# Squared-ReLU MLP: last store in two halves on two queues, w2 in three loads, last w1 loads merged

## Chip, cores, metric

One Trainium2 chip, one core, bfloat16. The metric is device time in microseconds (us). Times are quoted as the median of a kernel's runs. Every ratio is the mean time of one kernel's fast runs over the mean of the other's fast runs of the same rounds on the same chip, so it is not quite the ratio of the medians quoted beside it. "Span" is the time from the first to the last instruction in a profile; it is about 2 us shorter than the timed value. PE is TensorE; SPq and ACTq are the DMA queues of SyncE and ScalarE. A DMA is *issued* by its queue and has *landed* when all its bytes are in place, as its semaphore tells.

## The reference

```python
B, S, D, F = 1, 2048, 576, 4608
def reference(x, w1, b1, w2, b2):
    h = einsum("bsd,df->bsf", x, w1) + b1
    r = where(h > 0, h, 0)
    h = r * r
    return einsum("bsf,fd->bsd", h, w2) + b2
```

## The kernel before

The sequence is cut into four blocks of 512 rows. D = 576 is 4.5 times 128, so most of the first matmul is done in pairs: one matmul on partitions 0 to 63 and one on partitions 64 to 127, for two different columns of w1. Such a pair of column tiles is called a *row tile* here; there are 16. A row tile needs 18 matmuls (9 pairs), about 1.94 us (the first twelve run from 9.50 to 32.81 us in the profile).

w1 for these tiles is loaded in pieces. Each load fills 64 partitions, the lower or the upper half, and all are issued in order on SyncE's queue:

```python
    w1_v = w1.rearrange("(c p) f -> p c f", p=H)          # H = 64
    def load_w1(eng, h, j0, j1):
        keep(eng.dma_start(out=w1_h[h * H:(h + 1) * H, :, j0 * P:j1 * P],
                      in_=w1_v[:, :, GW + h * FH + j0 * P:GW + h * FH + j1 * P]))
    # ... cut ...
    W2CH = 18
    def load_w2(c):
        keep(nc.sync.dma_start(out=w2_sb[:, c * W2CH:(c + 1) * W2CH, :],
                               in_=w2_view[:, c * W2CH:(c + 1) * W2CH, :]))
    # ... cut ...
    for (j0, j1) in [(0, 1), (1, 2), (2, 4), (4, 6), (6, 8), (8, 10), (10, 12)]:
        load_w1(nc.sync, 0, j0, j1)
        load_w1(nc.sync, 1, j0, j1)
    load_xT(1)                                  # DMA transposes of x, block 1
    for (j0, j1) in [(12, 14), (14, 16)]:       # four loads of 288 KB
        load_w1(nc.sync, 0, j0, j1)
        load_w1(nc.sync, 1, j0, j1)
    # ... cut: b2 as a column (b2_col) and as rows (b2_bc) ...
    for c in range(2):
        load_w2(c)
    load_xT(2)
    alloc_hT(0)
    a_full(0, "k_outer")
    a_rows(0, 12, 1)                            # row tiles 0 to 15 of block 0
```

The end of the kernel stores the last 128 rows in two column pieces; only the second, 128 x 128 (32 KB), is stored after all other work:

```python
                keep(nc.vector.tensor_tensor(out=o_sb[:, d0:d1], in0=po[:, 0:d1 - d0], in1=b2_bc[:, d0:d1], op=ALU.add))
                keep(nc.sync.dma_start(out=out2[rt * P:(rt + 1) * P, d0:d1], in_=o_sb[:, d0:d1]))
```

## Time and profile before

| what | value |
|---|---|
| time, median of the first 3 runs (of 6 with those beside the changed kernel) | 290.89 us (290.85) |
| span of the profile | 288.7 us |
| PE busy | 284.6 us, 99% |
| last add ends | 286.42 us |
| tail after it | 2.3 us |

From the page of the kernel before, busy times by engine, and the chain that ended last by engine:

```profile
PE 284.6 (99%) x2027; PEld 138.9 (48%) x2032; DVE 78.6 (27%) x177; ACT 96.5 (33%) x152; POOL 0.9 (0%) x7
...
PE 97%; DMA 1%; SPq 0%; issue 0%; DVE 0%
```

TensorE bounds the kernel: it is busy for 284.6 of 288.7 us. So a DMA matters here only where PE waits for it, or after PE has finished.

The timeline of TensorE around the start of row tile 12 in block 0, kernel before. Columns: start in us, duration in us, engine, line, operation, output and inputs, shapes, count. L181 is the lower matmul of a pair, L183 the upper:

```profile
32.60 0.38 PE L181 MATMUL ph<-xTw,w_h 64*128 64x512 bf16 x1
32.60 0.38 PE L183 MATMUL ph<-xTw,w_h 64*128 64x512 bf16 x1
32.81 0.38 PE L181 MATMUL ph<-xTw,w_h 64*128 64x512 bf16 x1
32.82 0.38 PE L183 MATMUL ph<-xTw,w_h 64*128 64x512 bf16 x1
33.03 0.38 PE L181 MATMUL ph<-xTw,w_h 64*128 64x512 bf16 x1
```

Pairs start every 0.215 us. Tile 12 begins at 32.81 without a gap.

The timeline of SyncE's queue at the same place (issue times of DMAs; the four w1 loads are one merged row):

```profile
23.88 2.65 SPq L82 DMA_DIRECT2D w_h<-in_w_dram  x4
26.58 1.06 SPq L285 DMA_DIRECT2D b_col<-in_b_dram  x1
27.68 1.62 SPq L288 DMA_DIRECT2D b_bc<-in_b_dram  x1
```

The same four loads by tile (the issue's duration in ns, min/median/max, and starts; then the time from issue to landing):

```profile
L82 SPq DMA_DIRECT2D w_h<-in_w_dram x4: 609/636/638, 23.9 to 25.9; - x4
...
DMA to landing us min/median/max: 6.7/7.0/7.2
```

The trace has a landing for the last three of the four: 31.2, 32.4 and 32.9 us (start of issue plus time to landing). While they flow, between 26 and 30 us, the DMAs move 258 GB/s. The columns of this view: the stretch, its length, busy us (and instructions) of PE, weight loads, VectorE, ScalarE and GpSimd, the granted clock, the DMA engines' share, GB/s:

```profile
26.00:30.00 4.00, 4.00 (x40) 1.76 (x38) 1.82 (x5) 2.65 (x5) 0.00 (x0) 1.00 1.17 258
```

The timeline of the end, kernel before:

```profile
286.13 0.29 DVE L274 TENSOR_TENSOR o_sb<-po,b_bc 128x128 bf16<-128x128 f32 x1 [1.52 <-PE po L272]
286.45 0.33 SPq L275 DMA_DIRECT2D out_dram<-o_sb  x1
```

The store landed 1.5 us after its issue began; the closing semaphores bring the end to 288.7 us.

### The profile page before, as it was taken

The page shows a single profiled execution, that of the slowest core. Times are in us where ns is not written, and L with a number is a line of the kernel's source. Part 1 is how long each engine was busy: PE and PEld are TensorE (multiplying, and loading weights), DVE is VectorE, ACT ScalarE, POOL GpSimd, SP SyncE. Part 2 cuts the span into 40 slices and gives each one's busy share as a digit, 9 for nine tenths or more (in the row PEclk, how much of TensorE's full clock was granted, in tenths as well). Part 3 has the DMA queues.
Part 4 walks back from the last instruction along what each step waited for, and adds up shares of the span by engine and source line. Part 5 has one row for each costly group of instructions (what it writes and reads, how often), then busy time and mean ns, then how long its engine had stood idle before and what let it go on. Part 6 is the DMA issues. An engine that isn't in the chain of part 4 may idle for free.

```text
span 288.7 us, 4690 instructions
## 1 busy us (share of the span) xinstructions
PE 284.6 (99%) x2027; PEld 138.9 (48%) x2032; DVE 78.6 (27%) x177; ACT 96.5 (33%) x152; POOL 0.9 (0%) x7
## 2 busy tenths in 40 slices
PE   8999999999999999999999999999999999999996
PEld 5544444444444555555544444444444455555555
DVE  3444544444500200000025444444440001100001
ACT  3666666666500000000027666666670000000000
POOL 0000000000000000000000000000000000000000
PEclk9999999999999999999999999999999999999999
DMA  6999999600001100000000000000000110000000
GB/s 198 236 244 197 265 388 246 94 0 2 0 18 36 37 16 18 16 16 18 16 16 2 1 2 0 2 0 2 0 2 0 36 39 16 16 16 19 32 17 18
DMA packets 31573, 16.59 MB, mean 57 GB/s; under 512 B 15552, under 2 KB 31552, under 8 KB 31552
## 3 DMA queue, kind: packets, MB, share of 16 engines
q1 hardware_dynamic: 30928, 15.72, 22.3%
q10 hardware_dynamic: 624, 0.57, 0.7%
q8 instruction: 16, 0.26, 0.4%
q14 instruction: 5, 0.04, 0.0%
HBM read 11.43 MB, written 2.36 MB: 48 GB/s over the span
## 4 chain that ended last, share of the span: by engine, by line
PE 97%; DMA 1%; SPq 0%; issue 0%; DVE 0%
PE ph L181 42%; PE po L272 38%; PE pt L253 11%; PE pn L202 4%; DMA w1n<-in_w_dram 1%; PE pn L217 1%; PE ph L183 1%; PE pn L196 1%; SPq L72 0%; DVE o_sb L274 0%; PE b1T_ps L159 0%; PE pn L198 0%
## 5 line engine op out<-in xcount | busy, mean ns | idle before, releaser
L181 PE MATMUL ph<-xTw,w_h 64*128 64x512 bf16 x576 | 124.6, 376 | 0.0
L183 PE MATMUL ph<-xTw,w_h 64*128 64x512 bf16 x576 | 124.6, 376 | 0.0
L272 PE MATMUL po<-w_sb,hT 128*128 128x448 bf16 (+2 forms) x612 | 109.4, 341 | 0.0
L169 ACT ACTIVATE r<-ph,b1T 128x512 bf16<-128x512 f32 x128 | 81.1, 685 | 41.6 <-PE ph L183 41.6
L181 PEld LDWEIGHTS <-w_h 64*128 64x128 bf16 x576 | 54.1, 94 | 68.3
L272 PEld LDWEIGHTS <-hT 128*128 128x128 bf16 x612 | 58.5, 98 | 51.0
L170 DVE TENSOR_TENSOR hT<-r 128x512 bf16<-128x512 bf16 x144 | 61.2, 426 | 76.9 <-ACT r L169 76.9
L183 PEld LDWEIGHTS <-w_h 64*128 64x128 bf16 x576 | 54.1, 94 | 0.0
L274 DVE TENSOR_TENSOR o_sb<-po,b_bc 128x448 bf16<-128x448 f32 (+2 forms) x17 | 10.2, 597 | 125.8 <-PE po L272 125.8
L253 PE MATMUL pt<-hT,w_sb 128*128 128x512 bf16 x142 | 31.3, 379 | 0.1
L169 ACT ACTIVATE r<-pn,b1T 128x512 bf16<-128x512 f32 x16 | 10.3, 688 | 62.0 <-PE pn L198 60.6
L253 PEld LDWEIGHTS <-w_sb 128*128 128x128 bf16 x144 | 14.1, 98 | 17.0
L256 ACT ACTIVATE oT<-pt,b2T 128x512 bf16<-128x512 f32 x4 | 2.7, 687 | 28.3 <-PE pt L253 28.3
L202 PE MATMUL pn<-xTw,w1n 128*128 128x512 bf16 x45 | 10.4, 379 | 0.4 <-issue 0.3
L202 PEld LDWEIGHTS <-w1n 128*128 128x128 bf16 x48 | 4.5, 98 | 6.0 <-issue 0.8
L217 PE MATMUL pn<-xTw,w1n 128*128 128x256 bf16 x32 | 3.7, 273 | 0.1
L63 PE MATMUL wps<-const-bfloat16-1.0 128*128 128x512 bf16 (+1 forms) x7 | 2.9, 597 | 0.8 <-PEq L328 0.8
L217 PEld LDWEIGHTS <-w1n 128*128 128x128 bf16 x32 | 3.0, 98 | 0.6 <-DMA w1n<-in_w_dram 0.3
L115 DVE COPY xTw<-xTw 64x2048 bf16<-64x2048 bf16 x4 | 2.8, 690 | 0.6 <-ACT xTw L152 0.5
L116 DVE COPY xTw<-xTw 64x2048 bf16<-64x2048 bf16 x4 | 2.8, 688 | 0.1
L196 PE MATMUL pn<-xTw,w1n 64*128 64x512 bf16 x8 | 2.4, 379 | 0.0
L198 PE MATMUL pn<-xTw,w1n 64*128 64x512 bf16 x8 | 2.4, 379 | 0.0
(21 smaller groups left out, 10.5 us busy)
## 6 DMA issues: line engine op xcount, KB each, us to landing
w_sb<-in_w_dram SPq DMA_DIRECT2D x2, 2592.0 KB, 15.2
w_h<-in_w_dram SPq DMA_DIRECT2D x14, 288.0 KB, 6.6
out_dram<-o_sb SPq DMA_DIRECT2D x15, 112.0 KB, 1.7
w_h<-in_w_dram SPq DMA_DIRECT2D x4, 144.0 KB, 3.2
out_dram<-ot SPq DMA_DIRECT2D x4, 128.0 KB, 2.0
x_sb<-in_x_dram ACTq DMA_DIRECT2D x2, 144.0 KB, 3.0
x_sb<-in_x_dram SPq DMA_DIRECT2D x2, 144.0 KB, 3.0
w1n<-in_w_dram ACTq DMA_DIRECT2D x2, 128.0 KB, 3.6
```

The source lines that it names most:

```text
L63: keep(nc.tensor.matmul(wps[:, 0:n], lhsT=ones[:, 0:P], rhs=ones[:, 0:n], start=True, stop=True))
L115: keep(nc.vector.tensor_copy(out=xT[0:H, SPC:SPC + 4, :], in_=xT[H:P, E3:E3 + 4, :]))
L169: keep(nc.scalar.activation(out=r[:], in_=bank[:], func=ACT.Relu, bias=b1T[:, ft:ft + 1], scale=1.0))
L170: keep(nc.vector.tensor_tensor(out=hTs[sb][:, ft, :], in0=r[:], in1=r[:], op=ALU.mult))
L181: keep(nc.tensor.matmul(bx[:], lhsT=w1_h[0:H, LO_C[i], jc], rhs=xT[0:H, LO_W[i], :], start=(i == 0), stop=(i == NC - 1)))
L183: keep(nc.tensor.matmul(by[:], lhsT=w1_h[H:P, UP_C[i], jc], rhs=xT[H:P, UP_W[i], :], start=(i == 0), stop=(i == NC - 1)))
L196: keep(nc.tensor.matmul(banks[2 * i][:], lhsT=w1n8[0:H, 2 * i * P:(2 * i + 1) * P], rhs=xT[0:H, SPC, :], start=start, stop=stop, skip_grou ...
L202: keep(nc.tensor.matmul(banks[g][:], lhsT=w1n[:, k, g * P:(g + 1) * P], rhs=xT[:, O + k, :], start=start, stop=stop))
L217: keep(nc.tensor.matmul(banks[g][:, hc], lhsT=w1n[:, k, g * P:(g + 1) * P], rhs=xT[:, O + k, hc], start=(h == 0 and k == 0), stop=False, s ...
L253: keep(nc.tensor.matmul(pt[:], lhsT=w2_sb[:, ft, DM:D], rhs=hT[:, ft, :], start=(i == 0), stop=(i == NFT - 1)))
L272: keep(nc.tensor.matmul(po[:, 0:d1 - d0], lhsT=hT[:, ft, jj * P:(jj + 1) * P], rhs=w2_sb[:, ft, d0:d1], start=(i == 0), stop=(i == NFT - 1)))
L274: keep(nc.vector.tensor_tensor(out=o_sb[:, d0:d1], in0=po[:, 0:d1 - d0], in1=b2_bc[:, d0:d1], op=ALU.add))
```

## The change

Intent: issue fewer and larger w1 loads, spread w2 over three loads, and let two queues share the last store.

```diff
-    W2CH = 18
+    W2CH = 12
@@ last store
-                keep(nc.sync.dma_start(out=out2[rt * P:(rt + 1) * P, d0:d1], in_=o_sb[:, d0:d1]))
+                if last and rt == S // P - 1 and d1 == DM:
+                    for h, eng in enumerate((nc.sync, nc.scalar)):
+                        rows = slice(rt * P + h * H, rt * P + (h + 1) * H)
+                        keep(eng.dma_start(out=out2[rows, d0:d1], in_=o_sb[h * H:(h + 1) * H, d0:d1]))
+                else:
+                    keep(nc.sync.dma_start(out=out2[rt * P:(rt + 1) * P, d0:d1], in_=o_sb[:, d0:d1]))
@@ loads
-    for (j0, j1) in [(12, 14), (14, 16)]:
+    for (j0, j1) in [(12, 16)]:
         load_w1(nc.sync, 0, j0, j1)
         load_w1(nc.sync, 1, j0, j1)
@@
-    for c in range(2):
+    for c in range(3):
         load_w2(c)
```

## The prediction

> **What bounds the kernel now.** TensorE. The engine summary gives PE 284.6 us busy of a 288.7 us span (99%); the chain of waits puts 97% on PE and 1% on a DMA (first weight loads, 1.7 to 5.4 us). In the timeline matmuls follow one another every 0.215 us from 9.5 us on; the list of waits shows no PE wait on a DMA after 5.4 us. The last add ends at 286.42 us; then comes a tail of 2.3 us: the store is issued at 286.45 (0.33 us on SyncE's queue), lands 1.5 us after its issue began (the tile's DMA view), near 287.95, and closing semaphores take it to 288.7.
>
> The change touches DMAs only: it can gain only in that tail, and lose only by making PE wait.
>
> **1. Last store split (128 x 128, 32 KB).** Nearly all of the 1.5 us is fixed: stores of 112 KB land in 1.7 us. The DMA engines are busy 15% of the one microsecond in which this store moves. Two halves move the same bytes. [...] ScalarE is idle then, so the halves start together. But the two 64-partition loads of 64 KB took 0.58 us to issue, against 0.44 for 128-partition loads of 128 KB, and the end now waits for two landings. Estimate: +0.05 us, between -0.1 and +0.3.
>
> **2. w1 row tiles 12 to 15 in two loads of 576 KB instead of four of 288 KB.** The only place where PE could be made to wait. The four are issued from 23.88 to 26.52 us and land at about 30.6, 31.7, 32.4 and 32.9 us. Row tile 12 starts on PE at 32.81 us; it needs only the first two, with 1.1 us to spare. Merged, it needs all; landing as now, PE would wait about 0.1 us. But contiguous runs grow from 512 to 1024 bytes. With the DMA engines full, the 512-byte phase moves 234 to 292 GB/s (26 to 30 us) and the 1152-byte rows of w2 366 to 390. At an estimated 340 GB/s the 1.18 MB that start flowing at 26 us take 3.5 us instead of 4.5 to 5, so the last lands near 31 to 32 us. Expected PE wait 0; at worst about 0.5 us. SyncE saves about 1.3 us of issue, worth nothing.
>
> **3. w2 in three loads of 1.73 MB instead of two of 2.6 MB.** Now landed at about 41.2 and 48.2 us; the first matmul that reads w2 runs at 75.4. One issue more (0.4 us), same bytes and rows. Worth 0.
>
> **Sum.** 290.89 + 0.05 (tail) + 0.05 (small chance of a wait at tile 12) = 291.0 us, range 290.3 to 291.7, mostly the spread of the runs before (290.7 to 291.53). Chances: faster by over 2% 0.5%, within 2% 98.5%, slower by over 2% 1%.
>
> **What would show it.** Right: PE busy and chain the same within 0.5 us; row tile 12's first matmul at about 32.8 us without a wait; both w1 loads landed before it; w2 landed before 50 us; two stores near 286.5, each landing in 1.4 to 1.7 us, span ending 2.2 to 2.5 us after the last add. Wrong: a PE gap before tile 12; a tail under 2.1 us (halves do land sooner) or over 2.7.
>
> **What would make it wrong.** Merged loads landing after 33.3 us[...]; other waits reordered by the new number of transfers.

The sum as forecast: 290.89 + 0.05 + 0.05 = 291.0 us (290.99).

## The result

292.03 us median of 6 runs (291.65 to 292.75), against 290.85 (290.7 to 291.53) before: ratio 1.0038, 95% interval 1.0022 to 1.0054. That is about 1.1 us slower. It is within 2%, as forecast, but it lies above the forecast range of 290.3 to 291.7.

The page after, busy by engine and the chain that ended last:

```profile
PE 285.3 (98%) x2032; PEld 139.1 (48%) x2032; DVE 78.6 (27%) x177; ACT 96.5 (33%) x152; POOL 1.0 (0%) x7
...
PE 87%; SPq 6%; DMA 4%; issue 0%; ACTq 0%; DVE 0%
```

The chain no longer runs through PE alone: it now passes through SyncE's queue and a DMA.

TensorE at row tile 12, after. The bracket is idle time before the instruction and what ended it:

```profile
32.66 0.38 PE L181 MATMUL ph<-xTw,w_h 64*128 64x512 bf16 x1
32.67 0.38 PE L183 MATMUL ph<-xTw,w_h 64*128 64x512 bf16 x1
32.88 0.38 PE L181 MATMUL ph<-xTw,w_h 64*128 64x512 bf16 x1
33.74 0.39 PE L183 MATMUL ph<-xTw,w_h 64*128 64x512 bf16 x1 [0.49 <-DMA w_h<-in_w_dram]
33.75 0.39 PE L181 MATMUL ph<-xTw,w_h 64*128 64x512 bf16 x1
```

The upper matmul of the first pair should have started with its lower partner at 32.88. It started at 33.74: **0.86 us lost**. The bracket shows only 0.49, because it counts from the modelled end of the matmul before; start-to-start distances are the safer reading.

SyncE's queue, after:

```profile
24.21 1.29 SPq L82 DMA_DIRECT2D w_h<-in_w_dram  x2
25.54 0.63 SPq L290 DMA_DIRECT2D b_col<-in_b_dram  x1
26.22 0.61 SPq L293 DMA_DIRECT2D b_bc<-in_b_dram  x1
```

The second merged load was issued at 24.86 and took 8.8 us, so it landed at 33.7 us, when PE resumed:

```profile
L82 SPq DMA_DIRECT2D w_h<-in_w_dram x1: 633/633/633, 24.9 to 24.9; - x1
...
DMA to landing us min/median/max: 8.8/8.8/8.8
```

The loads did not move faster than before's four, as the prediction had hoped, but slower:

```profile
26.00:30.00 4.00, 4.00 (x40) 1.82 (x38) 1.79 (x5) 2.65 (x5) 0.00 (x0) 1.00 0.99 222
```

The end, after:

```profile
287.06 0.29 DVE L274 TENSOR_TENSOR o_sb<-po,b_bc 128x128 bf16<-128x128 f32 x1 [1.52 <-PE po L272]
287.38 0.56 SPq L278 DMA_DIRECT2D out_dram<-o_sb  x1
287.39 0.56 ACTq L278 DMA_DIRECT2D out_dram<-o_sb  x1
```

Each issue takes 0.56 us instead of 0.33. Both landings, from one view:

```profile
DMA to landing us min/median/max: 1.8/1.9/2.1
```

The SyncE half lands after 1.8 us, the ScalarE half after 2.1, and the span ends at 290.3: a tail of 3.0 us instead of 2.3.

So the profiled runs differ by 1.6 us (290.3 against 288.7), made of 0.86 at tile 12, about 0.65 in the tail, and 0.07 in the start-up. The medians differ by 1.2 us. That fits waits that vary from run to run, but only one run of this kernel was profiled. Two of the signs that the prediction had named as "wrong" are there: a PE gap before tile 12 and a tail over 2.7 us.

### The profile page after: what moved, and what is told of

It is laid out like the page before. It is cut to its first block, busy times and chain, and to the rows that moved or that the text cites. A ratio compares the mean times of both kernels' runs of the same rounds, so it can differ in the third digit from the quotient of the medians.

```text
span 290.3 us, 4696 instructions
## 1 busy us (share of the span) xinstructions
PE 285.3 (98%) x2032; PEld 139.1 (48%) x2032; DVE 78.6 (27%) x177; ACT 96.5 (33%) x152; POOL 1.0 (0%) x7
## 4 chain that ended last, share of the span: by engine, by line
PE 87%; SPq 6%; DMA 4%; issue 0%; ACTq 0%; DVE 0%
PE po L272 38%; PE ph L181 21%; PE ph L183 14%; PE pt L253 11%; SPq L82 4%; PE pn L202 4%; DMA w_h<-in_w_dram 3%; SPq L122 2%; DMA w1n<-in_w_dram 1%; SPq L123 0%; PE pn L196 0%; ACTq L72 0%; PE pn L198 0%; DVE o_sb L274 0%
```

## The experiments

Each kernel is the kernel before with only the edit shown, except where said. "Tail" is always the span's end minus the end of the last add.

### One part at a time

**Split store alone** (only the store hunk of the change).

> The kernel before with the last store alone split. Theory T (the split store itself costs): the end comes about 2.95 us after the last add instead of 2.28, so the kernel is 0.5 to 0.7 us slower than before, and no wait of PE on a w1 load. Rival (the loss is all in the loads): tail 2.3 us, time within 0.15 us of before.

Measured: 291.54 us against 291.01, ratio 1.0024 (1.0011 to 1.0037). The tail was 3.0 us; PE waited for no w1 load. So the split store by itself costs about 0.6 us. The rival fell.

**Merged w1 alone** (only the `(12, 16)` hunk).

> The kernel before with the last w1 loads alone merged. Theory W (tile 12 now waits for both merged loads): the upper load lands at 33.3 to 33.9 us, PE waits 0.5 to 1.0 us before row tile 12, the kernel is 0.4 to 0.9 us slower than before, tail unchanged at 2.3 us. Rival (the wait in the one profile of after was an accident of that run): no wait in the profile, time within 0.15 us of before.

Measured: 291.32 us against 291.01, ratio 1.0024 (1.0009 to 1.0039). The ratio is carried by two runs of six (292.39 and 292.04); the other four lie at 291.25 to 291.35. In the profile the upper load landed at 34.4 us and PE lost 0.9 us at tile 12. The tail is unchanged: the store lands after 1.5 us. Part of the profiled run's excess is not this wait: its row phase began at 10.18 us, 0.68 later than before's 9.50. The wait is there in all three profiles of kernels with these merged loads (0.86, 0.93 and, further below, 0.34 us), and its size varies.

**w2 in three loads alone** (only `W2CH` and `range`).

> The kernel before with w2 alone in three loads. Every theory so far: time within 0.15 us of before, w2 landed before 50 us, no PE wait. If instead the new number of transfers shifts other waits, a PE wait shows and the time moves by more than 0.3 us.

Measured: 291.01 us against 291.01, ratio 1.0007 (0.9995 to 1.0020). No effect shown, and w2 never made PE wait.

**Merged w1 loads issued early, w2 in three** (the store as before).

```diff
-    load_xT(1)
-    for (j0, j1) in [(12, 14), (14, 16)]:
+    for (j0, j1) in [(12, 16)]:
         load_w1(nc.sync, 0, j0, j1)
         load_w1(nc.sync, 1, j0, j1)
+    load_xT(1)
```

> w1 merged into the same two 576 KB loads, but issued ahead of the x transposes of block 1, and w2 in three loads; the last store as before. Theory W: the loads now land near 26 us, long before tile 12 at 32.8 us, so no PE wait and time within 0.15 us of before, although the loads are as large as in after. Rival (large loads disturb PE by themselves, or the three w2 loads do): still 0.4 us or more slower.

Measured: 290.97 us against 291.01, ratio 1.0003 (0.9991 to 1.0015). The loads landed by 27.7 us (not 26) and PE did not wait for them. So these two loads of 576 KB did no harm here, landed about 5 us before the time at which tile 12 starts in before (32.81). This version is as fast as the kernel before, not faster: before had no such wait to remove.

### The w1 loads: what tile 12 waits for, and why they land late

**Tile 12 alone in a small first pair.**

```diff
-    for (j0, j1) in [(12, 14), (14, 16)]:
+    for (j0, j1) in [(12, 13), (13, 16)]:
```

> Tile 12 alone in the first pair of loads (144 KB each), tiles 13 to 15 in the second pair (432 KB each): as many bytes and loads as before. Theory W (tile 12 waits for bytes it does not need): tile 12's pair lands near 29 to 30 us, no PE wait before tile 12; tile 13 starts 1.94 us later, near 34.8, and the second pair has landed by 34.3 whether grouping slows it or not, so no wait at all, time within 0.15 us of before. If the second pair lands after 34.8, PE waits there instead.

Measured: tile 12's pair landed at 29.6 us, the second pair at 34.3, and PE waited for neither. So tile 12's wait is a matter of grain: the merged loads make it wait for tiles 13 to 15. The time was 291.27 against 290.77, ratio 1.0015 (1.0000 to 1.0030), more than expected. In this profile the row phase itself began 0.84 us later than in before's (10.34 instead of 9.50), so the excess of that run came from the start-up, not from these loads.

**Same four loads, both lower ones first.**

```diff
-    for (j0, j1) in [(12, 14), (14, 16)]:
-        load_w1(nc.sync, 0, j0, j1)
-        load_w1(nc.sync, 1, j0, j1)
+    for h in range(2):
+        load_w1(nc.sync, h, 12, 14)
+        load_w1(nc.sync, h, 14, 16)
```

> The four 288 KB w1 loads of before, reordered: both lower ones (partitions 0 to 63) first, then both upper ones; runs of 512 bytes as before, tail as before. Theory G (grouping all traffic on one half of the partitions is what makes the merged loads slow): the last of the four lands at 33.5 us or later, as the merged ones did (33.7 and 34.4), not at 32.5 to 33.1 as in the unmerged runs so far; the third, which tile 12 needs, lands near 33, so PE waits 0 to 0.6 us. Theory R (the 1024-byte packets are slow): the last lands at 32.5 to 33.1 and PE does not wait.

Measured: the loads landed at 31.1 (second), 32.7 (third) and 33.9 us (fourth), as theory G asks; but alternating loads also landed at 33.7 us in one profile (the first column-split store below). PE did not wait, but the row phase happened to start late (10.56 us, so tile 12 came near 33.9). Time 291.00 against 290.77, ratio 1.0002 (0.9986 to 1.0019).

**Runs of 1024 bytes, but four alternating loads.** Each load takes tiles 12 to 15 and only some of the nine 64-row pieces of w1.

```diff
+    def load_w1c(eng, h, j0, j1, c0, c1):
+        keep(eng.dma_start(out=w1_h[h * H:(h + 1) * H, c0:c1, j0 * P:j1 * P],
+                      in_=w1_v[:, c0:c1, GW + h * FH + j0 * P:GW + h * FH + j1 * P]))
@@
-    for (j0, j1) in [(12, 14), (14, 16)]:
-        load_w1(nc.sync, 0, j0, j1)
-        load_w1(nc.sync, 1, j0, j1)
+    for (c0, c1) in [(0, 4), (4, NC)]:
+        load_w1c(nc.sync, 0, 12, 16, c0, c1)
+        load_w1c(nc.sync, 1, 12, 16, c0, c1)
```

> Runs of 1024 bytes as in the merged loads, but four loads again that alternate lower, upper, lower, upper, split by rows of w1 instead of by tile; tile 12 needs all four. Theory G: the alternation restores the rate, the last lands at 33.0 us or earlier, PE waits 0 to 0.3 us. Theory R: the last lands at 33.6 or later as with the merged ones, PE waits 0.6 us or more.

Measured: the last landed at 33.2 us, between the two expectations, and PE did not wait. Counted from the landing of the x transposes just ahead of them (26.9 us), the loads took 6.3 us, which is no longer than unmerged loads take (see below). Time 291.11 against 290.77, ratio 1.0008 (0.9993 to 1.0023).

**w2 in 64-partition loads**, as a probe: same rows of 1152 bytes, only half the partitions per load.

```diff
-        keep(nc.sync.dma_start(out=w2_sb[:, c * W2CH:(c + 1) * W2CH, :], in_=w2_view[:, c * W2CH:(c + 1) * W2CH, :]))
+        for h in range(2):
+            hp = slice(h * H, (h + 1) * H)
+            keep(nc.sync.dma_start(out=w2_sb[hp, c * W2CH:(c + 1) * W2CH, :], in_=w2_view[hp, c * W2CH:(c + 1) * W2CH, :]))
```

> w2 is loaded in four loads of 64 partitions by 18 row tiles (1.3 MB each) instead of two of 128 partitions; same 1152-byte rows; nothing waits for w2 until 75 us. Theory P (a load that writes only 64 partitions moves slower): the w2 phase runs at 200 to 250 GB/s instead of 366 to 390 and w2 lands near 52 to 56 us instead of 48. Rival (w1 is slow because of its source rows, 9216 bytes apart, or its many short runs): w2 still moves at 366 to 390 GB/s and lands by 49 us.

Busy times of stretches of the w2 phase, kernel before. As above, the last two columns are the DMA engines' share and GB/s:

```profile
36.00:40.00 4.00, 4.00 (x40) 1.81 (x38) 2.21 (x6) 2.65 (x5) 0.00 (x0) 1.00 1.09 391
40.00:44.00 4.00, 4.00 (x40) 1.79 (x38) 1.70 (x4) 2.64 (x5) 0.00 (x0) 1.00 1.08 384
```

The same stretches with w2 in halves:

```profile
36.00:40.00 4.00, 4.00 (x42) 1.80 (x38) 2.23 (x5) 2.64 (x6) 0.00 (x0) 1.00 1.08 215
40.00:44.00 4.00, 4.00 (x40) 1.80 (x38) 1.81 (x5) 2.64 (x5) 0.00 (x0) 1.00 1.08 206
```

The DMA engines look equally busy (share 1.08 to 1.09 in both; it adds up the times of all packets, so it can pass 1), but move 206 to 215 GB/s instead of 384 to 391. w2 landed at 59.3 us, later than even theory P expected. So w2 in loads that write only 64 partitions moved at a little over half the rate (one run). Why, no run shows. The four short w1 loads of before, which also write 64 partitions each, moved faster than that (258 GB/s), so the count of partitions is not the whole of it. They change halves every 288 KB, the w2 loads every 1.3 MB; whether that is the difference, the runs do not settle.

**Merged w1 with nothing behind it.** b2, w2 and the x transposes of block 2 move into row tile 12 and wait for a small VectorE write.

```diff
+    def late_loads():
+        keep(nc.vector.memset(b2_col[:], 0.0))
+        # the loads of b2_col, b2_bc, w2 and x block 2, moved here unchanged
@@ in a_rows, first block only
             if j == dup_at:
+                late_loads()
                 dup_windows(dup_sb)
@@
-    for (j0, j1) in [(12, 14), (14, 16)]:
+    for (j0, j1) in [(12, 16)]:
```

> w1 merged as in after, but everything that was queued behind it (b2, w2, the x transposes of block 2) is held back until row tile 11 is done, near 34.5 us, by a small VectorE write that the b2 load must wait for. Theory B (the traffic behind competes with the slowest part): the merged loads land by 32.8 us, no PE wait before tile 12. Theory P: they still move at 200 to 240 GB/s and land at 33.2 us or later, PE waits 0.4 us or more unless the row phase happened to start late.

Measured: the upper load landed at 33.0 us, 0.2 us later than theory B and 0.2 us earlier than theory P had asked for; PE still lost 0.34 us at tile 12. Busy times of seven one-microsecond stretches of this run (last two columns: DMA share and GB/s):

```profile
26.00:27.00 1.00, 1.00 (x12) 0.49 (x10) 0.70 (x2) 0.40 (x1) 0.00 (x0) 1.00 0.75 199
27.00:28.00 1.00, 1.00 (x14) 0.43 (x10) 0.20 (x1) 0.93 (x2) 0.00 (x0) 1.00 1.18 283
28.00:29.00 1.00, 1.00 (x12) 0.44 (x10) 0.64 (x2) 0.34 (x1) 0.00 (x0) 1.00 1.03 200
29.00:30.00 1.00, 1.00 (x12) 0.49 (x10) 0.26 (x1) 0.98 (x2) 0.00 (x0) 1.00 1.12 233
30.00:31.00 1.00, 1.00 (x14) 0.41 (x10) 0.59 (x2) 0.32 (x2) 0.00 (x0) 1.00 1.04 193
31.00:32.00 1.00, 1.00 (x12) 0.47 (x10) 0.32 (x1) 1.00 (x2) 0.00 (x0) 1.00 0.15 30
32.00:33.00 1.00, 1.00 (x11) 0.29 (x5) 0.53 (x2) 0.32 (x2) 0.00 (x0) 1.00 0.07 23
```

With nothing behind them the loads still moved at 193 to 283 GB/s, 222 on the mean of the first five rows, and after the bulk had ended near 31 us a thin rest of 23 to 30 GB/s took two more microseconds. So traffic behind the loads is not needed for them to be slow or to end late. Whether it adds something stays open. Time 291.12 against 290.85, ratio 1.0010 (0.9996 to 1.0025).

The landings in all profiles, counted from the landing of the x transposes (L123 in before) ahead of the w1 loads, because the start-up shifts whole runs (the row phase began at 9.50 us in before, at 10.56 in the reordered loads):

| w1 loads for tiles 12 to 15 | profiles | last w1 landing, us after the transposes |
|---|---|---|
| four, alternating halves, 512-byte runs | 10 | 6.0 to 7.5, mean 6.7 |
| four, alternating, 1024-byte runs | 1 | 6.3 |
| four, both lower halves first | 1 | 7.4 |
| two, merged | 3 | 7.1, 7.8, 8.0 |

(The kernel with tile 12 alone in the first pair, 6.8 us, is left out.) The merged loads land about 1 us later than the mean of the first row, but the ranges overlap. The packets, which the traces keep with their sizes, separate them better: nine tenths of these w1 bytes had moved 3.8 to 4.5 us after the transposes in the ten profiles of the first row (mean 4.2), but only 4.8 to 4.9 us after them in the three merged ones. The last twentieth straggles over 0.8 to 2.3 us in all fifteen profiles, merged or not, so the slow end is no effect of merging.

By the same count the second row has 4.2 us and the third 4.4, both inside the first row's range. As the two kernels that were to isolate the order have one profile each, "grouping one half's traffic is slower than alternating" (theory G) is not settled. What speaks for it is the second row: with the run length of the merged loads, but alternating, it is as fast as the first.

### The last store

**Whole store on ScalarE's queue.**

```diff
+                if last and rt == S // P - 1 and d1 == DM:
+                    keep(nc.scalar.dma_start(out=out2[rt * P:(rt + 1) * P, d0:d1], in_=o_sb[:, d0:d1]))
+                else:                                              # ... cut: the old line
```

> The last store whole (128 partitions) but issued on ScalarE's queue. Theory Q (the second queue is what costs, by being slow after a long idle time): issue or landing longer than SyncE's 0.33 and 1.5 us, tail 0.3 us or more longer than before. Theory S (the 64-partition shape costs): issue 0.33 us, landing 1.5, tail within 0.1 us of before.

Measured: issue 0.38 us, landing 1.5, tail 2.4 us. Theory Q fell: the second queue was not slow here. Time 291.22 against 290.77, ratio 1.0012 (0.9997 to 1.0027), so no difference is shown, with nothing in the tail to explain more than 0.1 us.

**Two column halves on two queues** (128 partitions by 64 columns each), run twice.

```diff
+                    # ... cut: in the same `if` as the split store
+                    for h, eng in enumerate((nc.sync, nc.scalar)):
+                        e0 = d0 + h * H
+                        keep(eng.dma_start(out=out2[rt * P:(rt + 1) * P, e0:e0 + H], in_=o_sb[:, e0:e0 + H]))
```

> The last store split by columns instead of rows: 128 partitions by 64 columns on each of the two queues, at the same time. Theory S (the 64-partition shape costs): each issue takes 0.33 us and lands in about 1.5 us, tail within 0.15 us of before. Theory C (two stores at once cost, whatever their shape): landings of 1.8 to 2.1 us as in after, tail 0.4 us or more longer than before.

> The column-split store once more. If the 0.26% of the first time is a cost of the two stores: again 0.5 to 0.8 us slower than before. If it was chance (a PE wait on an early w1 load, which the profile of that run shows and which no part of the tail can cause): within 0.2 us of before.

Both profiles show issues of 0.33 and 0.38 us, landings of 1.4 and 1.6, and a tail of about 2.45 us: 0.1 more than a whole store (2.33 in before). The first time the kernel was timed at 291.56 against 290.90, ratio 1.0026 (1.0011 to 1.0041), which the tail cannot explain. The profile of that run shows PE stopped elsewhere, at row tile 2, by an *early* w1 load:

```profile
13.37 0.38 PE L181 MATMUL ph<-xTw,w_h 64*128 64x512 bf16 x1
14.10 0.39 PE L183 MATMUL ph<-xTw,w_h 64*128 64x512 bf16 x1 [0.36 <-DMA w_h<-in_w_dram]
```

That is 0.73 us lost in a part of the program that this kernel has in common with before. The second time: 291.09 against 290.85, ratio 1.0005 (0.9992 to 1.0017). The first result was therefore not a cost of the two stores; that every run of it had such an early wait is not shown, since only one was profiled.

**Unchanged copy of before**, beside it.

> An unchanged copy of the kernel before, timed against itself: a ratio within 0.1% of 1. It shows how much two identical kernels differ by this method, and its profile gives a second look at the early w1 loads and the tail of before: tail 2.3 us after the last add, last w1 load landed at 32.4 to 33.8 us.

Measured: ratio 0.9999 (0.9984 to 1.0013), tail 2.3 us, last w1 landing 33.4 us.

**Only the lower half stored** (wrong result).

```diff
-                    for h, eng in enumerate((nc.sync, nc.scalar)):     # of the split store
+                    for h, eng in enumerate((nc.sync,)):
```

> Wrong result on purpose: only the lower half of the last store, 64 partitions on SyncE's queue, is made, and 64 rows by 128 columns of the output stay unwritten. Theory S: issue 0.56 us and landing 1.8 us although nothing runs beside it, tail 0.3 us longer than before. Theory C: issue 0.33, landing 1.5 or less, tail 2.3 us or less.

The lone store's record, by line. Columns: engine, operation, count, duration in ns (min/median/max), starts:

```profile
L278 SPq DMA_DIRECT2D out_dram<-o_sb x1: 565/565/565, 286.8 to 286.8; - x1
...
DMA to landing us min/median/max: 1.8/1.8/1.8
```

Tail 2.7 us. Half the bytes, alone, cost 0.3 us more than the whole store.

**Both row halves on SyncE's queue**, one after the other.

```diff
+                    for h, eng in enumerate((nc.sync, nc.sync)):       # of the split store
```

> Both 64-partition halves on SyncE's queue, one after the other. Theory S: two issues of 0.56 us, the second begins 0.6 us after the first and lands 1.8 us after that, so the tail is 0.8 to 1.0 us longer than before (3.1 to 3.3 us). Theory C (the pair on two queues disturb each other): issues of 0.33 us, the second lands 0.35 us later than one store, tail 2.6 us.

The same view for this kernel:

```profile
L278 SPq DMA_DIRECT2D out_dram<-o_sb x2: 560/572/583, 286.8 to 287.4; - x2
...
DMA to landing us min/median/max: 1.8/1.8/1.8
```

Tail 3.4 us. Time 292.11 against 290.90, ratio 1.0051 (1.0034 to 1.0068). Theory S held for the issues and landings; its tail (3.1 to 3.3 us) was 0.1 us too short. In these runs the shape of 64 partitions costs 0.23 us at the issue, and 0.3 us at the landing, which is counted from the start of the issue and so includes the 0.23. Two such halves at once on two queues cost another 0.3 us (tail 3.0), while two 128-partition halves at once cost 0.1. Why a 64-partition store issues more slowly no run shows.

No experiment gave a version faster than the kernel before.

## Why the prediction was wrong

- **What bounds the kernel, and w2:** right. PE stayed the bound, and w2 in three loads measured 1.0007 with an interval that includes 1.
- **Step 1, the tail ("+0.05 us, between -0.1 and +0.3"):** wrong in size: the split store alone measured about +0.6 us, twice the upper end. The prediction saw that 64-partition loads issue in 0.58 us against 0.44, and that the end waits for two landings, and then priced both at almost nothing. The lone half showed the shape to be worth 0.3 us, and the second queue beside it another 0.3.
- **Step 2, merged w1 ("the last lands near 31 to 32 us. Expected PE wait 0"):** wrong. The last landed at 33.7 (and 34.4, 33.0 in other merged kernels), and PE lost 0.86 us. The step that failed is the 340 GB/s; 222 GB/s was measured in its place (26 to 30 us). With 222 GB/s the prediction's own sum gives 5.3 us instead of 3.5 for the 1.18 MB, so a landing near 33 to 34 us instead of 31 to 32 (an estimate); 33.7 was measured. The 340 had been set near w2's rate, as if run length were what made w2 fast. But w2's loads write 128 partitions and w1's write 64; the probe took w2 to 206 to 215 GB/s with its row length unchanged. Runs of 1024 bytes in four alternating loads landed 6.3 us after the transposes, within the 6.0 to 7.5 of 512-byte runs, so longer runs gave no gain that one profile could show. That the merged loads fell below even before's 258 GB/s has no shown cause. Tile 12's new dependence on all the bytes was seen correctly; if the merged loads had landed at the mean of the unmerged ones (an estimate: 25.9 us for the transposes plus 6.7, or 32.6) they would just have met tile 12 at 32.9.
- **A reading error on the way:** "30.6" for the first load has no landing in the trace; 6.7 us belonged to the second load, so before's slack at tile 12 was 1.6 us, not 1.1. It did not decide the outcome.
- **The range:** the two mis-sized terms, 0.6 and up to 0.9 us, add to more than the range allowed; the median moved by 1.2.

## What to carry to other kernels

Before a rate taken from one load is used for another, compare how many partitions the two fill: here loads of 64 partitions instead of 128 took w2 from 384 to 391 GB/s down to 206 to 215, while w1's runs of 1024 bytes instead of 512 showed no gain (6.3 us, within the 6.0 to 7.5 of the shorter ones). The merged loads made tile 12 wait for bytes of tiles 13 to 15 (0.86 us lost in the profile of after, nothing with a small pair of its own): check each merged load against the time of its *first* reader, or issue it earlier (landed by 27.7 us, no wait). Splitting the last store by rows made each half take longer to land (1.8 us and more) than the whole had (1.5 us); with stores of 112 KB landing in 1.7 us, there was little in a 32 KB store that half the bytes could save.
